# Stage a of a Fourier layer on float16 parts of x, with x read twice

## The chip, the cores and the metric

The kernel runs on one core of one Trainium2 chip. The metric is the device time of the program in microseconds (us), the median of several runs. A core has a matrix engine (TensorE, in the profile PE, with its weight loads as PEld), a vector engine (DVE), an activation engine (ACT), a general engine (POOL), and a queue engine (SP) that only issues transfers here. Each engine works through its own instructions in order; where one needs another's result, it waits on a semaphore. Transfers between HBM and the on-chip memory (SBUF) run on 16 DMA engines and are issued from SP, ACT and POOL. Matmuls write to PSUM, from where ACT or DVE fetch their results.

## The reference

Two layers follow each other. The first works on `x` of 8 batches, 3072 rows, 256 columns; the second is a feed-forward layer on its output.

```python
X = np.fft.rfft(x, axis=1)
Yr = X.real @ w_r - X.imag @ w_i + b_r
Yi = X.real @ w_i + X.imag @ w_r + b_i
Y  = soft_threshold(Yr, 0.01) + 1j * soft_threshold(Yi, 0.01)
a  = np.fft.irfft(Y, n=3072, axis=1)                  # float32, 8 x 3072 x 256
h  = np.maximum(np.maximum(a @ w1, a @ w2), a @ w3)   # 768 columns
out = h @ w_out                                       # 24576 x 256
```

The feed-forward weights come as float64 and the result is float32.

## The kernel before

**Products in parts.** Most products are made on float16 parts: a value is scaled by a power of two, its rounded float16 is the high part, what is left the low part, and `mm3` (L131) makes three matmuls, high by high, high by low and low by high. The helpers `split` (L119) and `split_scaled` (L124) make the parts: ACT writes the high one, DVE subtracts it to get the low one. `split_scaled` takes a scale, which may be a number or a column of SBUF.

**The transform.** 3072 is 96 times 32. *Stage a* (L427) is the transform over 96: for each batch, `x` is read in eight loads of four of the 32 sub-sequences (`load_x`, L398; 96 partitions by 1024 columns, 384 KB). Each load makes two products of 96 rows by 512 columns with the 96 x 96 table. ACT fetches them into `aq`, and a transfer stores `aq` in a scratch tensor `a_d` in HBM. For batches 2 to 7, the parts of `x` are `xh` and `xl` in float32r, a 32-bit type of the matrix engine, and the table's parts `fh` and `fl` are float32r too; batches 0 and 1 use plain float32 with `fr`. *Stages b, w and q* take the result in 12 pieces per batch: `load_a` (L454) reads a piece `aj` from `a_d`, `split_a` (L459) makes its float16 parts with the scale `s0x`, then come the rest of the transform (`px`), the weights `w_r` and `w_i` (`py`), bias and threshold, and the first step back (`pz`), which is stored in the scratch `z_d`.

**The scales.** `s0x` depends on the largest absolute value of `x` in the batch. DVE takes it half a load at a time in `split_x` (L416), just ahead of that half's split, and at the end of `stage_a` of the batch's last load (L441 to L452) `exponent_of` makes one number of the 16 maxima: a reduction (`col`), a matmul that spreads it over the partitions (`pt`, L209), a second reduction, and small operations on a column of 128. `power` (L221) makes scales of it in three small operations each.

**The feed-forward loop.** It runs over 8 batches, 8 chunks `c` of 384 rows and 6 blocks `f` of 128 of the 768 columns. One turn is a slot: a batch has 48. In a slot, `up` makes 18 matmuls into three PSUM tiles `pu`, and ACT and DVE make the maximum of the three and its parts `hh`; `down` makes 9 matmuls into `pd` on the `hh` of the turn before. Once per chunk the next chunk's `zq` is read, split and transformed back (`pi`). Batch 0's transform runs ahead of the loop (0 to about 137 us); batch 1's runs within the loop's batch 0, and so on.

**What sets the order.** The work of the transform is put between the turns by a list of events with a position in slots (L688 to L702), and after each turn everything up to the present slot is called. For a load `q` with number `i` in batch `b`, the load of `x` is called at `p - 3`, the split at `p` and stage a at `p + 1`. For batches 2 to 7, `p` is 48 (b - 2) + 6 i + 2: its stage a runs two batches ahead of its feed-forward turns, and its stages b to q one batch ahead. Batch 1's pieces come every 2.2 slots, from slot 8 of the loop's batch 0 on, later batches' every 2.8. The order in which the calls are made gives each instruction its priority; a scheduler at build time makes each engine's list from it and gives out buffers, so that an instruction whose buffer isn't free is passed by others. `issue_after` (L401) keeps a load of `x` behind the last load of `aj` on SP's queue. `xq`, `xh` and `xl` have two buffers each.

Of the kernel before, what the change touches and what calls it, by code (L numbers as in the profile page):

```python
# [10 lines left out]
F32R = mybir.dt.float32r  # L11
F16 = mybir.dt.float16
U32 = mybir.dt.uint32
AX = mybir.AxisListType
AF = mybir.ActivationFunctionType
ALU = mybir.AluOpType
# [3 lines left out]
LAM = 0.01  # L20
SB, SG = 10, 20
T_SCALE, Y_SCALE, H_SCALE, Q_SCALE = 2.0**-15, 2.0**-14, 2.0**-22, 2.0**12


def dft_tables():
# [68 lines left out]
def fourier_maxout_kernel(  # L94
    ctx: ExitStack, tc: tile.TileContext, x, w_r, w_i, b_r, b_i, w1, w2, w3, w_out, fa, ga, mb, mq, ident, out
):
    nc = tc.nc
    NB, S, D = x.shape
    FF = w1.shape[1]
    P = 128  # L100
    N1, N2 = 96, 32
    KD = D // P
    NF = FF // P
    NQ = 4
    NCH = N2 // NQ
    NT = NQ * N1
    NJP = 12
    SLOTS = NCH * NF
    NATIVE = 2 * NCH

    const = ctx.enter_context(tc.tile_pool(name="const", bufs=1))
# [5 lines left out]
    st = {}  # L117

    def split(hi, lo, src):  # L119
        h = hi if hi.dtype == F16 else hi.bitcast(F32)  # L120
        nc.scalar.activation(out=hi, in_=src, func=AF.Copy)
        nc.vector.tensor_tensor(out=lo, in0=src, in1=h, op=ALU.subtract)

    def split_scaled(hi, lo, src, scale):  # L124
        h = hi if hi.dtype == F16 else hi.bitcast(F32)
        nc.scalar.activation(out=hi, in_=src, func=AF.Copy, scale=scale)  # L126
        nc.vector.scalar_tensor_tensor(  # L127
            out=lo, in0=src, scalar=scale, in1=h, op0=ALU.mult, op1=ALU.subtract
        )

    def mm3(o, lh, ll, rh, rl, start=True, stop=True, **kw):  # L131
        nc.tensor.matmul(o, lh, rh, start=start, stop=False, **kw)  # L132
        nc.tensor.matmul(o, lh, rl, start=False, stop=False, **kw)  # L133
        st["mm"] = nc.tensor.matmul(o, ll, rh, start=False, stop=stop, **kw)  # L134
# [4 lines left out]
    def ff_tile(name):  # L139
        tag = spare[0]  # L140
        if len(spare) > 1:
            spare.append(spare.pop(0))
        return ps.tile([P, 512], F32, name=name, tag=tag, bufs=2 if tag == "dn" else 3)

    fr = const.tile([N1, 96], F32, name="fr")
    fh = const.tile([N1, 96], F32R, name="fh")
    fl = const.tile([N1, 96], F32R, name="fl")
    qf = const.tile([P, 2, P], F32, name="qf")
    qh = const.tile([P, 2, P], F16, name="qh")
    ql = const.tile([P, 2, P], F16, name="ql")  # L150
# [16 lines left out]
    def quad_tile(name):  # L167
        return fft.tile([96, NQ * D], F32, name=name, bufs=1 if name == "zq" else 2)
# [4 lines left out]
    def x_tile(name):  # L173
        return fft.tile([P, 2 * D], F32, name=name, bufs=2)
# [25 lines left out]
    def small(name, dt=F32, bufs=1):  # L200
        return fft.tile([P, 1], dt, name=name, bufs=bufs)


    def exponent_of(mx, name, bits, mask, low):
        rows = mx.shape[0]
        col = small("col", bufs=2)
        nc.vector.tensor_reduce(out=col[0:rows], in_=mx, axis=AX.X, op=ALU.max)
        pt = ff_tile("pt")
        nc.tensor.matmul(  # L209
            pt[:, 0:rows], col[0:rows].broadcast_to([rows, P]), id_sb[0:rows, 0:rows],  # L210
            start=True, stop=True,
        )
        e = small("e" + name, U32, 2)
        nc.vector.tensor_reduce(out=e.bitcast(F32), in_=pt[:, 0:rows], axis=AX.X, op=ALU.max)
        nc.vector.tensor_scalar(
            out=e, in0=e, scalar1=bits, scalar2=mask, op0=ALU.logical_shift_right, op1=ALU.bitwise_and
        )
        nc.vector.tensor_scalar(out=e, in0=e, scalar1=low, scalar2=None, op0=ALU.max)
        return e

    def power(name, e, sign, add, bufs=3):  # L221
        t = small(name, U32, bufs)
        nc.vector.tensor_scalar(out=t, in0=e, scalar1=sign, scalar2=add, op0=ALU.mult, op1=ALU.add)
        nc.vector.tensor_scalar(out=t, in0=t, scalar1=255.0, scalar2=None, op0=ALU.min)
        nc.vector.tensor_scalar(out=t, in0=t, scalar1=23, scalar2=None, op0=ALU.logical_shift_left)
        return t.bitcast(F32)
# [157 lines left out]
    def batch(b, kind):  # L384
        if (b, kind) not in st:
            if kind in "az":
                st[b, kind] = dram.tile([96, N2, D], F32, name=kind + "_d")
            else:
                w = 2 * NCH if kind == "x" else NJP
                st[b, kind] = fft.tile([P, w], F32, name="mx" + kind, bufs=3)  # L390
        return st[b, kind]
# [6 lines left out]
    def load_x(q):  # L398
# [8 lines left out]
            pairs = [xq[:, i * 2 * D:(i + 1) * 2 * D] for i in range(2)]  # L407
        st["x", q] = pairs

    def split_x(q):  # L410
        b, q4 = divmod(q, NCH)
        pairs = st.pop(("x", q))
        parts = []
        for i, xp in enumerate(pairs):
            if b:
                nc.vector.tensor_reduce(  # L416
                    out=batch(b, "x")[0:N1, 2 * q4 + i:2 * q4 + i + 1], in_=xp, axis=AX.X,
                    op=ALU.max, apply_absolute_value=True,
                )
            if q >= NATIVE:  # L420
                xh, xl = (x_tile(n).bitcast(F32R)[0:N1] for n in ("xh", "xl"))
                split(xh, xl, xp)
                xp = xh, xl
            parts.append(xp)
        st["xs", q] = parts

    def stage_a(q):  # L427
        b, q4 = divmod(q, NCH)
        aq = first_quads[q] if q < NCH else quad_tile("aq")
        for i, xp in enumerate(st.pop(("xs", q))):  # L430
          with tc.issue_after(st["gate"]) if q >= NCH + 2 and q < NATIVE else nullcontext():
            pa = ff_tile("pa")
            if q < NATIVE:
                nc.tensor.matmul(pa[0:96], fr, xp, start=True, stop=True)  # L434
            else:
                mm3(pa[0:96], fh, fl, *xp)
            nc.scalar.activation(out=aq[:, i * 512:i * 512 + 512], in_=pa[0:96], func=AF.Copy)
        (nc.scalar if b else nc.gpsimd).dma_start(
            out=batch(b, "a")[:, q4 * NQ:(q4 + 1) * NQ, :], in_=aq.rearrange("p (n d) -> p n d", n=NQ)
        )  # L440
        if b and q4 == NCH - 1:  # L441
            low, add = st["lim", "x"]
            e = exponent_of(st.pop((b, "x"))[0:N1], "x", 23, 0xFF, low)
            st[b, "sx"] = power("s0x", e, -1.0, 261.0), power("s1x", e, 1.0, add)


            m = small("mv", bufs=2)
            nc.vector.tensor_scalar(
                out=m, in0=e, scalar1=add, scalar2=st["eb"], op0=ALU.add, op1=ALU.max
            )  # L450
            nc.vector.tensor_scalar(out=m, in0=m, scalar1=230.0, scalar2=None, op0=ALU.min)
            st[b, "sv"] = power("s0v", m, -1.0, 231.0), power("s1v", m, 1.0, 11.0)  # L452

    def load_a(k):  # L454
        first = ("vl", 3) if k < NJP and k % 5 > 1 else ("aj", 2)
# [3 lines left out]
    def split_a(k):  # L459
        if k < NJP:  # L460
            return
        aj = st.pop(("a", k))
        ah = fft.tile([P, 2, D], F16, name="ah")
        al = fft.tile([P, 2, D], F16, name="al")
        split_scaled(ah, al, aj, st[k // NJP, "sx"][0])
        st["as", k] = [ah, al]


# [215 lines left out]
    def at(pos, fn, i, k=None, n=None):  # L684
        if n is None or 0 <= k < n:
            events.append((pos, len(events), fn, i))

    for q in range(NCH + 2, NB * NCH):  # L688
        b, i = divmod(q, NCH)
        p = i if b == 1 else (b - 2) * SLOTS + NF * i + 2  # L690
        at(p - 3, load_x, q)
        at(p, split_x, q)
        at(p + 1, stage_a, q)
    for b in range(1, NB):
        for k in range(-2, NJP + 1):
            p = 8 + 2.2 * (k + 2) if b == 1 else (b - 1) * SLOTS + 2.8 * (k + 2)
            for d, fn, i in (
                (0, load_a, k + 2), (0, split_a, k + 1), (1.6, finish_w, k - 1), (1, stage_b, k + 1),
                (3.2, stage_q, k - 1), (2, stage_w, k), (2.4, stage_w2, k),
            ):  # L700
                at(p + d, fn, b * NJP + i, i, NJP)
# [82 lines left out]
                nc.scalar.dma_start(out=out_v[b, c, t], in_=o)  # L784

    nc.sync.dma_start(out=fr, in_=fa)
    split(fh, fl, fr)

    def load_blocks(i):
        nc.sync.dma_start(out=mb_sb[:, :, 6 * i:6 * i + 6], in_=mb[:, :, 6 * i:6 * i + 6])  # L790
# [20 lines left out]
    for q in range(NCH):  # L811
        split_x(q)
        stage_a(q)
# [53 lines left out]
    for q in (NCH, NCH + 1):  # L867
        split_x(q)
        stage_a(q)
# [67 lines left out]
```

## Time and profile before

| | |
|---|---|
| three runs | 2063.78, 2065.49, 2070.24 us (median 2065.49) |
| the profiled execution | 2070.11 us, its span 2068.3 us |
| granted TensorE clock | 0.995 in the mean |
| busy, share of the span | PE 99%, PEld 69%, DVE 75%, ACT 50%, POOL 1% |
| HBM | 87.14 MB read, 75.50 MB written, 79 GB/s |
| loads of `xq` | 58 of 384 KB, 4.0 us from issue to landing in the median |
| `pa` on float32r | 288 matmuls of 96x96 by 512 columns |

A profile shows one execution: each instruction with its line, engine, tiles (out<-in), start and duration. A row of a group has the count, the busy time, the mean duration, then the idle time of the engine just before such instructions and what ended it ("<-DVE c L758 1.1" is 1.1 us that ended with DVE's result of line 758). Matmuls overlap, so their durations add up to more than the time; what counts is how far apart they start. "issue" is waiting for which the profile shows no cause. A row of the waits has the total, the number and the longest. A wait is put down to what came last.

### The profile page before, as it was taken

The numbers are of one execution on the slowest core, as the hardware profiler recorded it, in microseconds if no ns is written. First come the engines' busy times: TensorE is split into PE (matmuls) and PEld (weight loads), VectorE is DVE, ScalarE is ACT, GpSimd is POOL, SyncE is SP. The second block draws the span as 40 slices with busy tenths as digits, with TensorE's granted clock in tenths as the row PEclk, the third lists the DMA queues.
The fourth block names the chain that finished last, engine by engine and source line by source line (L and its number), as shares of the span: only waits on it lengthen the run. The fifth ranks groups of instructions, "written<-read, shape, count | busy, mean of one in ns | idle before, by whom it ended". The sixth has DMA issues, their size and how long they took to land.

```text
span 2068.3 us, 38435 instructions
## 1 busy us (share of the span) xinstructions
PE 2040.7 (99%) x15500; PEld 1431.4 (69%) x15500; DVE 1547.9 (75%) x3043; ACT 1035.0 (50%) x2051; POOL 27.6 (1%) x79
## 2 busy tenths in 40 slices
PE   8999999999999999999999999999999999999998
PEld 5756766677776767767776777767777777776666
DVE  3987897678867888678886788767887578865543
ACT  4755554455545555455554455445554445433333
POOL 1000000000000000000000000000000000000000
PEclk9999999999999999999999999999999999999999
DMA  9454221322213222223213222132221212111100
GB/s 311 141 155 123 90 70 52 107 68 89 75 52 100 79 84 62 65 83 92 85 60 97 62 78 87 47 100 72 86 74 44 77 52 67 42 47 32 34 30 23
DMA packets 106694, 165.13 MB, mean 80 GB/s; under 512 B 9795, under 2 KB 85059, under 8 KB 106419
## 3 DMA queue, kind: packets, MB, share of 16 engines
q1 hardware_dynamic: 45347, 86.69, 14.4%
q10 hardware_dynamic: 60032, 72.37, 10.6%
q0 software_dynamic: 1136, 3.61, 0.5%
q8 instruction: 121, 1.98, 0.4%
q14 instruction: 58, 0.48, 0.1%
HBM read 87.14 MB, written 75.50 MB: 79 GB/s over the span
## 4 chain that ended last, share of the span: by engine, by line
PE 82%; DVE 10%; DMA 3%; ACT 2%; issue 2%; ACTq 0%; SPq 0%; DVEq 0%
PE pu L134 16%; PE pu L132 16%; PE pu L133 16%; PE pd L134 5%; PE pd L132 5%; PE pd L133 5%; PE py L132 2%; PE py L133 2%; PE py L134 2%; DMA xq<-in_x_dram 2%; DVE u L620 1%; PE pi L132 1%; PE pa L434 1%; DVE h L760 1%; PE pa L133 1%
## 5 line engine op out<-in xcount | busy, mean ns | idle before, releaser
L132 PE MATMUL pu<-yh,wuh 128*128 128x384 f16 x2304 | 752.6, 327 | 2.2 <-DVE c L758 1.1
L133 PE MATMUL pu<-yl,wuh 128*128 128x384 f16 x2304 | 751.7, 326 | 0.0
L134 PE MATMUL pu<-yh,wul 128*128 128x384 f16 x2304 | 751.7, 326 | 0.0
L126 ACT ACTIVATE hh<-h 128x384 f16<-128x384 f32 x384 | 200.4, 522 | 512.3 <-DVE h L760 509.8
L134 PEld LDWEIGHTS <-wul 128*128 128x128 f16 x2304 | 225.5, 98 | 148.9 <-issue 1.1
L132 PEld LDWEIGHTS <-wuh 128*128 128x128 f16 x2304 | 225.9, 98 | 143.4 <-issue 14.7
L133 PEld LDWEIGHTS <-wuh 128*128 128x128 f16 x2304 | 225.9, 98 | 135.1 <-issue 5.8
L758 DVE TENSOR_TENSOR c<-pu,c 128x384 f32<-128x384 f32 x384 | 212.5, 554 | 136.8 <-PE pu L134 76.3
L127 DVE SCALAR_TENSOR_TENSOR hh<-h,hh 128x384 f16<-128x384 f32 x384 | 213.6, 556 | 135.3 <-ACT hh L126 132.0
L134 PE MATMUL pd<-woh,hh 128*128 128x256 f16 x1152 | 313.6, 273 | 0.9 <-DVE hh L127 0.8
L132 PE MATMUL pd<-woh,hh 128*128 128x256 f16 x1152 | 313.9, 273 | 0.4 <-ACT hh L126 0.3
L133 PE MATMUL pd<-wol,hh 128*128 128x256 f16 x1152 | 313.8, 273 | 0.0
L760 DVE TENSOR_TENSOR h<-pu,c 128x384 f32<-128x384 f32 x384 | 212.7, 554 | 45.6 <-PE pu L134 33.8
L757 ACT ACTIVATE c<-pu 128x384 f32<-128x384 f32 x384 | 186.0, 484 | 102.7 <-PE pu L134 98.6
L620 DVE SCALAR_TENSOR_TENSOR u<-py,s1x,cs 64x256 f32<-64x256 f32 x308 | 148.5, 482 | 40.9 <-ACT cs L631 30.9
L132 PE MATMUL py<-wch,tt 128*128 128x256 f16 x504 | 137.4, 273 | 0.4 <-DVE yl L127 0.4
L134 PE MATMUL py<-wch,tt 128*128 128x256 f16 x504 | 137.4, 273 | 0.0
L133 PE MATMUL py<-wcl,tt 128*128 128x256 f16 x504 | 137.4, 273 | 0.0
L132 PEld LDWEIGHTS <-hh 128*128 128x128 f16 x1152 | 112.7, 98 | 34.3 <-ACT hh L126 1.0
L133 PEld LDWEIGHTS <-hh 128*128 128x128 f16 x1152 | 112.7, 98 | 33.4
L783 ACT ACTIVATE o<-pd,s1u 128x256 f32<-128x256 f32 x192 | 83.6, 469 | 90.9 <-PE pd L134 53.3
L134 PEld LDWEIGHTS <-hh 128*128 128x128 f16 x1152 | 112.7, 98 | 15.3 <-DVE hh L127 2.0
(205 smaller groups left out, 2889.6 us busy)
## 6 DMA issues: line engine op xcount, KB each, us to landing
aj<-a_d SPq DMA_DIRECT2D x96, 256.0 KB, 2.8
z_d<-zs ACTq DMA_DIRECT2D x96, 256.0 KB, 2.1
out_dram<-o ACTq DMA_DIRECT2D x192, 128.0 KB, 2.1
zq<-z_d SPq DMA_DIRECT2D x63, 384.0 KB, 3.5
xq<-in_x_dram SPq DMA_DIRECT2D x58, 384.0 KB, 4.0
a_d<-aq ACTq DMA_DIRECT2D x56, 384.0 KB, 3.0
rw<-in_moe_w_dram SPq DMA_DIRECT2D x6, 768.0 KB, 9.4
xr<-in_x_dram SPq DMA_DIRECT2D x6, 384.0 KB, 11.4
```

The costliest lines, as they stand in the source:

```text
L126: nc.scalar.activation(out=hi, in_=src, func=AF.Copy, scale=scale)
L127: nc.vector.scalar_tensor_tensor(out=lo, in0=src, scalar=scale, in1=h, op0=ALU.mult, op1=ALU.subtract)
L132: nc.tensor.matmul(o, lh, rh, start=start, stop=False, **kw)
L133: nc.tensor.matmul(o, lh, rl, start=False, stop=False, **kw)
L134: st["mm"] = nc.tensor.matmul(o, ll, rh, start=False, stop=stop, **kw)
L434: nc.tensor.matmul(pa[0:96], fr, xp, start=True, stop=True)
L620: nc.vector.scalar_tensor_tensor(out=u[64 * c:64 * c + 64, j], in0=pk[r], scalar=inv[r], in1=c1[r], op0=ALU.mult, op1=ALU.add,)
L757: nc.scalar.activation(out=c1, in_=pu[0], func=AF.Copy)
L758: nc.vector.tensor_tensor(out=c1, in0=pu[1], in1=c1, op=ALU.max)
L760: nc.vector.tensor_tensor(out=h32, in0=pu[2], in1=c1, op=ALU.max)
L783: nc.scalar.activation(out=o, in_=pd[t], func=AF.Copy, scale=st[b, "su"][1])
```

## The change

For batches 2 to 7, stage a works on float16 parts. The table's parts `fh` and `fl` become float16, made with a scale of 2^10. `xh` and `xl` become float16, made by `split_scaled` with a new scale `sx2` in a column, which needs the batch's maximum ahead of the first split. So `x` is read twice: once for the maximum (`load_x`, `largest_x`), and once more for the split. The two halves of a load take one buffer of the tiles `xh` and `xl` each, with high and low part side by side. For b of 3 to 7 the maximum is called at slot 48 (b - 3) + 6 i + 5, between the splits of the batch before, and its load three slots earlier. For batch 2 it is called at slots 8, 10, ... 22, and the split, which stood at slots 2, 8, ... 44, at 24.5, 27.4, ... 44.8. The scales of a batch (`scale_x`) are made behind the last maximum, not behind the last stage a. `aq` is fetched with a scale of 2^-17, so what lies in `a_d` is scaled already, and `aj` of batches 2 to 7 is split without one. Batches 0 and 1 stay on float32.

```diff
+A_SCALE, F_SCALE = 2.0**-17, 2.0**10
...
-    fh = const.tile([N1, 96], F32R, name="fh")
-    fl = const.tile([N1, 96], F32R, name="fl")
+    fh = const.tile([N1, 96], F16, name="fh")
+    fl = const.tile([N1, 96], F16, name="fl")
...
+    def largest_x(q):
+        b, q4 = divmod(q, NCH)
+        for i, xp in enumerate(st["x", q]):
+            nc.vector.tensor_reduce(
+                out=batch(b, "x")[0:N1, 2 * q4 + i:2 * q4 + i + 1], in_=xp, axis=AX.X,
+                op=ALU.max, apply_absolute_value=True,
+            )
+        if b > 1 and q4 == NCH - 1:
+            scale_x(b)
+
+    def scale_x(b):
+        low, add = st["lim", "x"]
+        e = exponent_of(st.pop((b, "x"))[0:N1], "x", 23, 0xFF, low)
+        st[b, "sx"] = power("s0x", e, -1.0, 261.0), power("s1x", e, 1.0, add)
+        if b > 1:
+            st[b, "sx2"] = power("s2x", e, -1.0, 268.0)
...
     def split_x(q):
         b, q4 = divmod(q, NCH)
-        pairs = st.pop(("x", q))
+        if b == 1:
+            largest_x(q)
         parts = []
-        for i, xp in enumerate(pairs):
-            if b:
-                nc.vector.tensor_reduce(
...
+        for i, xp in enumerate(st.pop(("x", q))):
             if q >= NATIVE:
-                xh, xl = (x_tile(n).bitcast(F32R)[0:N1] for n in ("xh", "xl"))
-                split(xh, xl, xp)
+                t = x_tile(("xh", "xl")[i]).bitcast(F16)[0:N1]
+                xh, xl = t[:, 0:2 * D], t[:, 2 * D:4 * D]
+                split_scaled(xh, xl, xp, st[b, "sx2"][0:N1])
                 xp = xh, xl
...
-            nc.scalar.activation(out=aq[:, i * 512:i * 512 + 512], in_=pa[0:96], func=AF.Copy)
+            nc.scalar.activation(
+                out=aq[:, i * 512:i * 512 + 512], in_=pa[0:96], func=AF.Copy,
+                scale=1.0 if q < NATIVE else A_SCALE,
+            )
...
-        split_scaled(ah, al, aj, st[k // NJP, "sx"][0])
+        if k // NJP > 1:
+            split(ah, al, aj)
+        else:
+            split_scaled(ah, al, aj, st[k // NJP, "sx"][0])
...
-        p = i if b == 1 else (b - 2) * SLOTS + NF * i + 2
+        p = i if b == 1 else 24.5 + 2.9 * i if b == 2 else (b - 2) * SLOTS + NF * i + 2
+        if b > 1:
+            m = 8 + 2 * i if b == 2 else (b - 3) * SLOTS + NF * i + 5
+            at(m - 3, load_x, q)
+            at(m, largest_x, q)
         at(p - 3, load_x, q)
         at(p, split_x, q)
         at(p + 1, stage_a, q)
...
-    split(fh, fl, fr)
+    split_scaled(fh, fl, fr, F_SCALE)
```

More of the change, by code (lines that the diff above doesn't have):

```diff
@@ L408, in load_x @@
         st["x", q] = pairs
+    def largest_x(q):
[13 more added lines that the diff above has]
+            st[b, "sx2"] = power("s2x", e, -1.0, 268.0)
+        m = small("mv", bufs=2)
+        nc.vector.tensor_scalar(
+            out=m, in0=e, scalar1=add, scalar2=st["eb"], op0=ALU.add, op1=ALU.max
+        )
+        nc.vector.tensor_scalar(out=m, in0=m, scalar1=230.0, scalar2=None, op0=ALU.min)
+        st[b, "sv"] = power("s0v", m, -1.0, 231.0), power("s1v", m, 1.0, 11.0)
     def split_x(q):
         b, q4 = divmod(q, NCH)
-        pairs = st.pop(("x", q))
+        if b == 1:
+            largest_x(q)
         parts = []
-        for i, xp in enumerate(pairs):
-            if b:
[L416 to L419, printed above, removed]
+        for i, xp in enumerate(st.pop(("x", q))):
             if q >= NATIVE:
-                xh, xl = (x_tile(n).bitcast(F32R)[0:N1] for n in ("xh", "xl"))
-                split(xh, xl, xp)
+                t = x_tile(("xh", "xl")[i]).bitcast(F16)[0:N1]
+                xh, xl = t[:, 0:2 * D], t[:, 2 * D:4 * D]
+                split_scaled(xh, xl, xp, st[b, "sx2"][0:N1])
                 xp = xh, xl
@@ L436, in stage_a @@
                 mm3(pa[0:96], fh, fl, *xp)
-            nc.scalar.activation(out=aq[:, i * 512:i * 512 + 512], in_=pa[0:96], func=AF.Copy)
+            nc.scalar.activation(
+                out=aq[:, i * 512:i * 512 + 512], in_=pa[0:96], func=AF.Copy,
+                scale=1.0 if q < NATIVE else A_SCALE,
+            )
         (nc.scalar if b else nc.gpsimd).dma_start(
@@ L440, in stage_a @@
         )
[L441 to L452, printed above, removed]
+        if b == 1 and q4 == NCH - 1:
+            scale_x(b)
     def load_a(k):
```

## The prediction

> **What bounds the kernel now.** I read the page's busy shares first, then the chain of waits, then the windows by batch, and last the groups and the timeline around stage a.
>
> ```profile
> span 2068.3 us, 38435 instructions
> PE 2040.7 (99%) x15500; PEld 1431.4 (69%) x15500; DVE 1547.9 (75%) x3043; ACT 1035.0 (50%) x2051; POOL 27.6 (1%) x79
> ...
> PE 82%; DVE 10%; DMA 3%; ACT 2%; issue 2%; ACTq 0%; SPq 0%; DVEq 0%
> ```
>
> TensorE has work in 99% of the span and is 82% of the chain that ended last; the 10% of DVE lie where a late DVE result came through to a matmul. So a second that leaves TensorE's queue is worth a second, and one that leaves or joins DVE, ACT or a DMA queue is worth something only where it makes TensorE wait. Where that happens is in the windows by batch of the feed-forward loop:
>
> ```profile
> 137.00:376.00 239.00, 234.26 (x1775) 161.68 (x1774) 190.81 (x374) 123.41 (x249) 2.16 (x8) 0.98 0.30 90
> 376.00:624.00 248.00, 247.63 (x1943) 175.54 (x1942) 195.55 (x379) 128.74 (x257) 2.91 (x8) 1.00 0.25 77
> ...
> 1371.00:1620.00 249.00, 248.23 (x1946) 175.64 (x1945) 194.62 (x376) 129.04 (x258) 2.12 (x8) 1.00 0.25 75
> ```
>
> The columns are length, then busy time of PE, PEld, DVE, ACT and POOL, the granted clock, the DMA share and GB/s. While the loop runs batch 0 (137 to 376) TensorE idles 239.00 - 234.26 = 4.7 us at a clock of 0.98; while it runs batches 1 and 5 it idles 0.4 and 0.8 us. From batch 1 on there are hardly any stalls to win; matmul time alone can be won there. In the first window both matter.
>
> **Part 1, the matmuls of stage a.** 48 loads of x (batches 2 to 7) give two products each, each of three matmuls of 512 columns: 288 matmuls, now on float32r, then on float16. What counts is their pace, start to start, in a run of them:
>
> ```profile
> 622.33 0.40 PE L133 MATMUL pa<-xl,fh 96*96 96x512 f32 x1
> 622.57 0.39 PE L134 MATMUL pa<-xh,fl 96*96 96x512 f32 x1
> 622.80 0.39 PE L132 MATMUL pa<-xh,fh 96*96 96x512 f32 x1
> 623.03 0.40 PE L133 MATMUL pa<-xl,fh 96*96 96x512 f32 x1
> 623.26 0.40 PE L134 MATMUL pa<-xh,fl 96*96 96x512 f32 x1
> ```
>
> ```profile
> 600.02 0.38 PE L132 MATMUL pz<-vp,qh 128*128 128x512 f16 x1
> 600.23 0.38 PE L133 MATMUL pz<-vp,qh 128*128 128x512 f16 x1
> 600.45 0.38 PE L134 MATMUL pz<-vp,ql 128*128 128x512 f16 x1
> 600.66 0.21 PE L132 MATMUL pi<-ga_sb,zh 96*128 96x96 f16 x1
> ```
>
> The float32r matmuls follow each other at (623.26 - 622.33) / 4 = 0.2325 us, float16 ones of as many columns at (600.66 - 600.02) / 3 = 0.2133 us. The difference, 0.0192 us, times 288 is **5.5 us** off TensorE's queue. Bounds: 0, if the pace of the 96-row, 96-column product isn't due to its type, and 5.5. The row nearest in type and columns is pz, so I take the whole.
>
> The Trainium skill, page "TensorE: Matmul & The Clock Gate", section "Wait — 56ns, not 53.3ns?", gives a warm matmul its columns over 2.4 GHz and some 2.5 ns, 215.7 ns for 512; pz in the trace has 213 ns at the 10 ns steps of the timeline, which agrees. By the page's figure the term would be 288 x 0.0168 = 4.8 us and the time 2059.3.
>
> The change of type also has an exit:
>
> ```profile
> 711.52 0.40 PE L134 MATMUL pa<-xh,fl 96*96 96x512 f32 x1
> ...
> 711.76 0.10 PEld L132 LDWEIGHTS <-ah 128*128 128x128 f16 x1 [0.30 <-issue]
> ...
> 711.95 0.22 PE L132 MATMUL px<-mb_all,ah 128*128 128x128 f16 x1
> ```
>
> ```profile
> L132 PEld LDWEIGHTS <-ah 128*128 128x128 f16 x336 | 32.9, 98 | 5.4 <-issue 1.5
> ```
>
> Behind the last float32r matmul the next weights are loaded only when it has streamed (711.76), where float16 weights are loaded a matmul ahead, and the next product starts 0.43 us after it in place of 0.2325: 0.19 us lost. The group's 1.5 us of "issue" at 0.30 each make 5 such places, **1.0 us**. The other 43 groups are followed by a longer product that hides most of it; I give them 0.01 each, **0.4 us** (an estimate, a tick of the timeline). Bounds of the exits: 0 to 1.4.
>
> **Part 2, the splits.** xh and xl become float16 with a scale that stands in a column; aj's split loses such a scale for 72 of its 84 pieces.
>
> ```profile
> L416 DVE TENSOR_REDUCE mxx<-xq 96x1 f32<-96x512 f32 x112 | 74.2, 675 | 17.7 <-DMA xq<-in_x_dram 17.5
> ...
> L122 DVE TENSOR_TENSOR xl<-xq,xh 96x512 fp32r<-96x512 f32 x96 | 65.2, 684 | 18.3 <-ACT xh L121 18.3
> L127 DVE SCALAR_TENSOR_TENSOR al<-aj,s0x,ah 128x512 f16<-128x512 f32 x84 | 62.7, 747 | 5.1 <-ACT ah L126 3.4
> ...
> L126 ACT ACTIVATE ah<-aj,s0x 128x512 f16<-128x512 f32 x84 | 60.0, 716 | 7.2 <-DMA aj<-a_d 4.8 <-PE px L133 2.3
> L121 ACT ACTIVATE xh<-xq 96x512 fp32r<-96x512 f32 x96 | 58.6, 620 | 3.8 <-DMA xq<-in_x_dram 3.8
> ```
>
> The scaled split of 512 elements costs 716 on ACT and 747 on DVE, the plain one 620 and 684. DVE: 96 x 63 ns more and 72 x 63 ns less, 1.5 us over six batches; ACT: 24 x 96 ns, 2.3 us. The maxima stay 96 of 675 ns. The new scale is three small operations per batch, like the one below:
>
> ```profile
> L224 DVE TENSOR_SCALAR s0x<-s0x x7: 148/150/152, 169.1 to 1621.7; 128x1 uint32<-128x1 uint32 x7
> ```
>
> 18 x 150 ns are 2.7 us. All of it lies under TensorE: DVE has 248.00 - 195.55 = 52 us free in a batch, ACT 119. I cost it at **nothing**; without the cover it would be the 1.5 + 2.7 us of DVE. The split of the 96 x 96 table at the start is one operation for one.
>
> **Part 3, what moves in time.** The maximum of batch b (3 to 7) moves from its split, a batch earlier (slots 5 to 47 of the 48 before). So from batch 1 on each window does as many maxima as before, three slots away from the splits instead of in one burst with them. The first window does batch 2's and batch 3's: 16 x 0.675 = 10.8 us more on DVE, 190.81 + 10.8 = 201.6 of 239, 84% in place of 80%. The last window with splits has 10.8 us less. The share is far from 100%, so on average nothing is due; locally see the rivals.
>
> Batch 2's splits move from slots 2, 8, ... 44 to 24.5, 27.4, ... 44.8. With them go the only two waits of stage a on TensorE's side worth speaking of:
>
> ```profile
> L132 PE MATMUL pa<-xh,fh 96*96 96x512 f32 x96 | 41.8, 437 | 3.5 <-ACT zs L675 2.4 <-DVE u L620 1.1
> ```
>
> ```profile
> 274.03 0.47 PE L132 MATMUL pa<-xh,fh 96*96 96x512 f32 x1 [2.37 <-ACT zs L675]
> ...
> 277.66 0.43 PE L134 MATMUL pu<-yh,wul 128*128 128x384 f16 x1
> 277.93 0.33 PE L132 MATMUL pu<-yh,wuh 128*128 128x384 f16 x1
> ```
>
> ```profile
> 260.00:280.00 20.00, 17.63 (x117) 11.29 (x115) 16.72 (x33) 10.50 (x21) 0.00 (x0) 0.91 0.19 60
> ```
>
> They are 3.5 us of idle time, and the longer one was followed by a halved clock (a mean of 0.91 over 20 us, 1.8 us lost; the durations fall back at 277.9). That makes 5.3 us. Whether eight denser places meet such waits no row shows: the lower bound is that both vanish, -5.3; the upper that more come, priced in the rivals. Two in eight is the only rate I have, so I take as many again: **0**.
>
> The scale's matmul pt now follows the last maximum at once, on TensorE's queue ahead of the next up products. It could wait there for DVE. The group says how that goes for the other scales, which are made so already:
>
> ```profile
> L209 PE MATMUL pt<-id_sb,col 128*128 128x128 f32 (+1 forms) x38 | 7.5, 285 | 0.1
> ```
>
> 0.1 us of waiting over 38 of them: I take **0**; the upper bound is six waits of the 1.1 us that DVE u cost above, 6.6 us.
>
> 48 more loads stand on SP's queue, behind them the loads of aj and zq, and the second load of x may keep ACT waiting as the first keeps DVE.
>
> ```profile
> xq<-in_x_dram SPq DMA_DIRECT2D x58, 384.0 KB, 4.0
> ```
>
> ```profile
> SPq L406 <- DVE xl L122: 206.2, 12, 27.8
> ```
>
> They are asked for three slots, some 15 us, ahead of use and land in 4.0. SP already stands up to 27.8 us before such a load for its buffer without a stall of that length anywhere on TensorE, and 48 x 384 KB over the 1480 us from 137 to 1620 add 13 GB/s to 77. The maxima's 17.5 us of waits for x stood on DVE; as much again on ACT would fall in its free half. **0**; without that cover it is a second 17.5 us.
>
> **The sum.** 5.5 + 1.0 + 0.4 = 6.9 us. The profiled execution took 2070.1 us (span 2068.3, 1.8 around it), so it would take 2063.2. It is the slow end of the runs shown; their median is 2065.5, and from that the forecast is **2058.6 us**, -0.33%.
>
> **The rivals.** *The stalls go too* (20%). Both waits of the first window belong to places that batch 2 leaves, and the burst of maximum and subtraction is parted: 6.9 + 5.3 = 12.2, 2053.3 us. Against it: the new places lie where batch 1's stages are densest.
>
> *It doesn't do what it says* (17%): the pace of 0.2325 belongs to 96 columns and 96 rows or to the reading of weights, not to the type. Then 0 to 1.4 remains, 2064 to 2065.5 us. For it: no row has a float16 product of 96 x 96 by 512. Against it: pa's 512 columns also last longer one by one than pz's, 403 ns against 363, and the type is what the two differ in beside 32 rows:
>
> ```profile
> L133 PE MATMUL pa<-xl,fh 96*96 96x512 f32 x96 | 38.7, 403 | 0.3 <-DVE xl L122 0.3
> ...
> L133 PE MATMUL pz<-vp,qh 128*128 128x512 f16 (+1 forms) x91 | 33.0, 363 | 0.0
> ```
>
> The Trainium skill, same page, section "Weight-path perf modes — Fast Weight Load (FWL) and DoubleRow", has the fast load for 128 columns of weights only, which these never have; no run so far shows it for float16.
>
> *DVE is too full in the first window* (13%, slower). Batch 2's places come every 2.9 slots while batch 1's products come every 2.2, and all share DVE:
>
> ```profile
> 200.00:220.00 20.00, 18.89 (x164) 13.51 (x162) 19.12 (x37) 10.83 (x22) 0.00 (x0) 1.00 0.26 74
> ...
> 280.00:300.00 20.00, 20.00 (x178) 14.92 (x177) 19.09 (x36) 12.06 (x24) 0.00 (x0) 1.00 0.36 107
> ```
>
> Where DVE is at 95% today, the window at 200 lost 1.1 us and that at 280 nothing. Each pa that then waits for its PSUM buffer behind a late zs costs 2.4 + 1.8 = 4.2 us with the clock's fall. The two of today cost 5.3; to eat the 6.9 it takes 12.2 / 4.2, three of the eight places. At five: 21.0 - 5.3 - 6.9 = +8.8, 2074.3 us. Against it: DVE goes to 84% only, and ends the window with slack. On the clock the Trainium skill, same page, section "What's actually happening", has it halved after an idle window of some 3.4 us; here 2.4 us of waiting were enough, and the measured row decides. By the page's length such a wait would cost no clock, and five would come to 12.0 - 5.3 - 6.9, 2065.3 us.
>
> **How the numbers follow.** Forecast 45%, own range 2055 to 2062; the rest beyond the rivals' 50%, 5%, is that pt or the x loads take some us off the gain. A measurement of this kernel can tell about 0.3%, 6.2 us: faster is under 2059.3, slower over 2071.7. The forecast is faster in some six of ten of its own cases (0.27), stalls that go are faster (0.20), and a little of the rest: 0.49. Slower is the third rival and a part of the rest: 0.14. The remaining 0.37 is no difference. The range from 2050 to 2068 leaves out the third rival's far part and the best tail.
>
> **What would show it.** pa on TensorE at 96x512 f16 with means near 363 and starts 0.213 apart (part 1); no 0.30 of "issue" at the weights that follow pa (exits); xh near 716, xl near 747, ah near 620, al near 684 (part 2); DVE near 202 us in the loop's first window, and the idle time of pa's first matmul there (part 3); pt's idle time near 0. The prediction is wrong if pa keeps its 0.23, or if TensorE's idle time in the first window leaves 3 to 7 us.

## The result

The changed kernel takes a median of 2117.3 us (2116.7 to 2121.0, 4 runs), the kernel before 2067.0 us on the same chip (2063.8 to 2070.2, 4 runs). The ratio is 1.0238, with a 95% interval of 1.0226 to 1.0251: it is **slower by 50 us**, where 2058.6 and a range of 2050 to 2068 were forecast.

The busy shares and the chain of waits of the changed kernel:

```profile
span 2119.2 us, 38519 instructions
PE 2056.9 (97%) x15500; PEld 1432.2 (68%) x15500; DVE 1548.5 (73%) x3061; ACT 1037.6 (49%) x2051; POOL 24.5 (1%) x79
...
PE 70%; DVE 13%; DMA 8%; ACT 4%; issue 3%; ACTq 1%; SPq 1%; DVEq 0%
```

DVE and ACT do no more than before (DVE 1548.5 against 1547.9 us, ACT 1037.6 against 1035.0), and TensorE has as many matmuls (15500). What has grown are the shares of DMA (3 to 8%) and DVE (10 to 13%) in the chain that ended last, at TensorE's cost (82 to 70%). The windows by batch, with the columns as in the prediction, and behind them 20 us in the middle of a batch:

```profile
137.00:376.00 239.00, 229.89 (x1747) 158.22 (x1748) 199.51 (x406) 124.52 (x246) 2.17 (x8) 0.99 0.40 116
376.00:624.00 248.00, 241.22 (x1868) 168.93 (x1867) 190.27 (x366) 125.15 (x249) 2.12 (x8) 0.98 0.29 86
624.00:873.00 249.00, 241.60 (x1859) 169.38 (x1858) 190.83 (x372) 125.19 (x248) 2.12 (x8) 0.98 0.30 89
1371.00:1620.00 249.00, 244.55 (x1899) 171.67 (x1898) 182.88 (x357) 127.90 (x253) 0.00 (x0) 0.99 0.25 75
...
770.00:790.00 20.00, 16.55 (x112) 11.02 (x113) 13.37 (x25) 10.31 (x20) 0.00 (x0) 0.83 0.18 54
```

In the windows of loop batches 0 to 5 TensorE now idles 4 to 10 us (before 0.3 to 4.7), and the granted clock is 0.98 to 0.99; before it was 0.98 in the first of them and 1.00 in the others. The loss lies in all the batches, not in the first window: from the first up product of one batch to that of the next, loop batches 0 to 5 took 270.8, 248.5, 249.3, 248.5, 249.8 and 249.2 us before, and 273.6, 259.1, 259.5, 261.8, 258.3 and 254.3 after. A wait of TensorE can be taken from the starts of two matmuls in a row, as the time beyond the usual step of their shape. Added up behind 200 us, the waits of over 0.25 us come to some 49 us (12 before), and 14 stretches of 3.4 us run at half the clock (1 before), which costs another 21 us (2 before). The products of stage a are some 5 us shorter. 37 + 19 - 5 = 51 us, and the spans differ by 50.9.

The waits that have grown, in the list of waits (in all, times, longest, in us), after:

```profile
DVE xh L128 <- ACT xh L127: 30.7, 25, 3.5
PE pi L133 <- DVE u L641: 24.9, 12, 4.0
ACT xh L127 <- DMA xq<-in_x_dram: 22.8, 11, 3.8
DVE mxx L414 <- DMA xq<-in_x_dram: 21.4, 24, 2.3
PE px L133 <- ACT zs L696: 9.1, 4, 3.0
```

and the same of before, where `px` waits for no `zs`:

```profile
DVE xl L122 <- ACT xh L121: 18.3, 36, 1.1
DVE mxx L416 <- DMA xq<-in_x_dram: 17.5, 18, 2.4
ACT xh L121 <- DMA xq<-in_x_dram: 3.8, 2, 2.3
PE pi L132 <- DVE u L620: 1.3, 3, 0.6
```

One of the longest is followed here in the changed kernel's timeline (start, duration, engine, line, operation; in brackets the idle time before it and what ended it):

```profile
765.32 0.38 SPq L475 DMA_DIRECT2D aj<-a_d  x1
765.79 0.42 SPq L407 DMA_DIRECT2D xq<-in_x_dram  x1
...
770.89 0.72 ACT L127 ACTIVATE xh<-xq,s2x 96x512 f16<-96x512 f32 x1 [3.38 <-DMA xq<-in_x_dram]
...
771.64 0.75 DVE L128 SCALAR_TENSOR_TENSOR xh<-xq,s2x,xh 96x512 f16<-96x512 f32 x1 [3.55 <-ACT xh L127]
772.32 1.99 DVE L641 SCALAR_TENSOR_TENSOR u<-py,s1x,cs 64x256 f32<-64x256 f32 x4
...
773.34 0.26 PE L133 MATMUL pi<-ga_sb,zh 96*128 96x96 f16 x1 [3.75 <-DVE u L641]
...
774.60 0.53 PE L133 MATMUL pu<-yh,wuh 128*128 128x384 f16 x1
...
780.30 0.33 PE L133 MATMUL pu<-yh,wuh 128*128 128x384 f16 x1
```

Read it from below. TensorE stands 3.75 us before `pi`, since `u` comes late; `u` stands on DVE's list behind the split `xh`, which waits for ACT's half of it, which waits for a load of x. That load was issued 5.1 us before, at once behind the load of `aj` (L402 ties it there, and `aj` waits for `al` to free its buffer). ACT and DVE work off their lists in order, so all that stands behind the split waits too, though it needs no x. Then the clock falls: `pu` lasts 0.53 us in place of 0.33, from 1.3 us before TensorE goes on until 778.9, and the window of 770 to 790 has a granted clock of 0.83.

### The profile page after: what moved, and what is told of

The parts are those of the page before. It is cut to its first block, busy times and chain, and to the rows that moved or that the text cites. A ratio compares the mean times of both kernels' runs of the same rounds, so it can differ in the third digit from the quotient of the medians.

```text
span 2119.2 us, 38519 instructions
## 1 busy us (share of the span) xinstructions
PE 2056.9 (97%) x15500; PEld 1432.2 (68%) x15500; DVE 1548.5 (73%) x3061; ACT 1037.6 (49%) x2051; POOL 24.5 (1%) x79
## 4 chain that ended last, share of the span: by engine, by line
PE 70%; DVE 13%; DMA 8%; ACT 4%; issue 3%; ACTq 1%; SPq 1%; DVEq 0%
PE pu L135 14%; PE pu L134 14%; PE pu L133 14%; PE pd L135 5%; PE pd L133 5%; PE pd L134 5%; DMA xq<-in_x_dram 4%; DVE u L641 2%; PE py L135 2%; PE py L133 2%; PE py L134 2%; DMA aj<-a_d 1%; DVE c L783 1%; DVE h L785 1%; DMA a_d<-aq 1%
```

## The experiments

Each is told with its edit (against the changed kernel, or against the one before where that is said), what was expected, and its median with that of the kernel before, run beside it. Behind it stand the ratio and its 95% interval.

**One read.** The first read of x and the maxima of batches 2 to 7 go; the scales are batch 1's, so that part of the computation is left out.

```diff
-        if b > 1:
-            st[b, "sx2"] = power("s2x", e, -1.0, 268.0)
+        st[b, "sx2"] = power("s2x", e, -1.0, 268.0)
...
+        for n in range(2, NB):
+            for name in ("sx", "sx2", "sv"):
+                st[n, name] = st[1, name]
...
-            at(m - 3, load_x, q)
-            at(m, largest_x, q)
```

> The changed kernel without the first read of x and without the maxima of batches 2 to 7, which this leaves out: the scales made for batch 1 serve for all. Stage a on float16, the scaled splits and their places stay. Theory Q (a load of x lands late because it stands on SP behind a load of aj, and ACT or DVE then stand in order before TensorE's next need): half of the late loads are gone and the buffers of xq serve one stream, so most of the 50 us go; 2060 to 2085 us, with waits of xh for the load left where it still stands behind aj. Rival D (DVE too full, or the scaled splits too long): the DVE work of the maxima, 65 us, is gone, so it falls below 2060 us as well, but xh no longer waits for anything. Rival F (the float16 products or the wait for the new scale cost the time): it stays near 2117 us.

2073.8 us against 2065.9, ratio 1.0035 (1.0022 to 1.0048). Some 42 of the 50 us go with the read and its maxima, and no wait behind 200 us brings a stretch at half the clock, but it isn't faster than before even with 96 maxima less. Waits of the same kind stay in this kernel's list:

```profile
ACT xh L127 <- DMA xq<-in_x_dram: 24.3, 16, 3.6
PE pi L133 <- DVE u L643: 10.6, 11, 2.8
```

So the second read isn't the whole of it: the splits still stand right behind their loads.

**No tie behind aj.** The loads of x of batches 2 to 7 are no longer kept behind that of `aj`.

```diff
-        with tc.issue_after(st["ld"].ins) if q >= NCH + 2 else nullcontext():
+        with tc.issue_after(st["ld"].ins) if NCH + 2 <= q < NATIVE else nullcontext():
```

> The changed kernel, where the loads of x of batches 2 to 7 are no longer tied behind the last load of aj on SP's queue; two buffers of xq as before. Theory Q: the loads go out when their buffer is free, some 5 us earlier at the place where one was issued at 765.8 us, and the five waits of pi of 3.7 to 4.2 us with the halved clock behind them go: 2058 to 2075 us. Rival B (two streams share two buffers, and that makes the load late): no more than a few us, 2105 to 2117 us. Rival D and F: 2117 us.

2081.3 against 2065.9, 1.0070 (1.0055 to 1.0085): some 35 of the 50 us come back with nothing left out and both reads in place. That is 6 us more than theory Q allowed. ACT's `xh` no longer appears as waiting for a load, and one stretch of half clock remains. The edit also lets the lists of SP, DVE and ACT come out in another order.

**Float32r, else as changed.** `fh`, `fl`, `xh` and `xl` go back to float32r, and with that to four buffers for a load: one of `xh` and one of `xl` for each half.

```diff
-    fh = const.tile([N1, 96], F16, name="fh")
-    fl = const.tile([N1, 96], F16, name="fl")
+    fh = const.tile([N1, 96], F32R, name="fh")
+    fl = const.tile([N1, 96], F32R, name="fl")
...
-                t = x_tile(("xh", "xl")[i]).bitcast(F16)[0:N1]
-                xh, xl = t[:, 0:2 * D], t[:, 2 * D:4 * D]
+                xh, xl = (x_tile(n).bitcast(F32R)[0:N1] for n in ("xh", "xl"))
```

> The changed kernel with the parts of x and of the table in float32r, and all else as changed: two reads, the places, the scale, aj split without one. Theory Q and rival B: the time stays high, 2117 us and the 5 to 7 us that the float16 products save, 2118 to 2130 us. Rival F (float16): back to 2067 us.

2087.4 against 2065.9, 1.0099 (1.0082 to 1.0116): 29 us less than the changed kernel, with *longer* products, where 2118 to 2130 was expected. The edit has two parts, the type and the buffers; the run below parts them.

**The second read in other buffers.** It goes to the eight raw buffers that hold x at the start, in place of the two of `xq`.

```diff
-    def load_x(q):
+    def load_split_x(q):
+        load_x(q, q >= NATIVE)
+
+    def load_x(q, again=False):
...
-            if 2 <= q < NCH:
+            if again or 2 <= q < NCH:
...
-        at(p - 3, load_x, q)
+        at(p - 3, load_split_x, q)
```

> The changed kernel, where the second read of x goes into the eight buffers of the tile raw, idle after the weights are made, so that the two reads share no buffer; the tie behind aj stays. Theory Q: a load still goes out only behind a load of aj, but an earlier one, where the missing buffer had held it to the next: part of the 50 us goes, 2070 to 2110 us. Rival B: all of it goes, 2055 to 2070 us. Rival D and F: 2117 us.

2125.9 against 2065.9, 1.0281 (1.0265 to 1.0296): no better, some 10 us worse, and above every time that was expected. The wait is the same one under another name:

```profile
ACT xh L127 <- DMA xr<-in_x_dram: 23.2, 10, 4.2
```

That two reads share two buffers of `xq` isn't the cause. With eight buffers at hand the load still stands behind `aj`.

**Float16, four buffers.** The changed kernel with its types, but each half of a load with one buffer of `xh` for its high part and one of `xl` for its low part, half of each unused.

```diff
-                t = x_tile(("xh", "xl")[i]).bitcast(F16)[0:N1]
-                xh, xl = t[:, 0:2 * D], t[:, 2 * D:4 * D]
+                xh, xl = (x_tile(n).bitcast(F16)[0:N1, 0:2 * D] for n in ("xh", "xl"))
```

> The changed kernel on float16, with the high part in a buffer of xh and the low part in one of xl for each half, as the kernel before has it, so that a load takes four buffers and not two; the lists of SP, ACT and DVE are then those of the run on float32r with two reads (2087.4 us). Theory P (the halved use of the buffers let the list put a split behind a load just issued, and the type has no part in it): 2087 less the 5 to 7 us of the products, 2079 to 2083 us. Rival F (float16 itself costs time): 2100 to 2117 us.

2085.5 against 2065.5, 1.0100 (1.0083 to 1.0117), as the float32r kernel with as many buffers (and 2.5 us above what was expected). The lists of SP, ACT and DVE are the same in these two, instruction by instruction, so those 29 to 30 us belong to **the buffers**, not to the type. The timeline of the float32r one shows what they do, at the place of the wait followed above:

```profile
742.88 0.41 SPq L407 DMA_DIRECT2D xq<-in_x_dram  x1
...
753.55 0.72 ACT L127 ACTIVATE xh<-xq,s2x 96x512 fp32r<-96x512 f32 x1
...
759.77 0.22 PE L133 MATMUL pi<-ga_sb,zh 96*128 96x96 f16 x1 [1.41 <-DVE u L640]
```

With two buffers of a name and two halves to a load, the next split has to wait until the last load's products are through, and the build-time list puts it late: 10.7 us behind its load, which has long landed (3.7 us is the median to landing). In the changed kernel a load takes one buffer of each name, so the other one is there for the next load, and the list puts the split earlier: 5.1 us behind a load that the tie has made late. Over all 48 loads for the splits (each matched to its split in the order of the calls), 23 splits of the changed kernel start within 6 us of their load's issue, 8.7 us in the median. With four buffers none does: 32 us in the median, 10 at least.

**Float16 by a fixed scale, in the kernel before.** x is read once, as before; `xh` and `xl` are float16 with a fixed scale of 2^10 in place of the batch's own, once with the halved buffers of the change (shown), and once with four. `fh` and `fl` become float16 by the same scale, and `aq` is fetched with 2^-20.

```diff
-                xh, xl = (x_tile(n).bitcast(F32R)[0:N1] for n in ("xh", "xl"))
-                split(xh, xl, xp)
+                t = x_tile(("xh", "xl")[i]).bitcast(F16)[0:N1]
+                xh, xl = t[:, 0:2 * D], t[:, 2 * D:4 * D]
+                split_scaled(xh, xl, xp, 2.0**10)
```

> The kernel before, with stage a of batches 2 to 7 on float16 parts alone: x is read once and its maximum taken at the split as before, and the parts are made with a fixed scale of 2^10 in place of one from the maximum, so it serves only for x of about this size (that part of the computation is left out). aj's split keeps its scale. If the products' pace is what float16 gives (0.2155 us in place of 0.232, and no exit), 288 products save 5 to 7 us and nothing moves: 2059 to 2062 us against 2066. If the two halves of a load, which now take one buffer of xh and xl each, let the splits run ahead to a load just landed, as theory Q has it for the changed kernel, waits of xh or of the maximum for the load grow and eat it: 2065 to 2085 us.

> The kernel before, with stage a of batches 2 to 7 on float16 parts by a fixed scale of 2^10 (so it serves only for x of about this size, that part of the computation is left out), x read once, and high and low part in a buffer of xh and xl each as before. The lists of SP, ACT and DVE are then in the order of the kernel before, instruction for instruction. Theory P: the products' pace and the exits alone change, 5 to 7 us less than before's 2066: 2058 to 2062 us. If float16 has a cost of its own that the lists don't show (the scaled split of DVE, the weights' loads): 2064 to 2075 us.

Halved: 2087.6 against 2065.5, 1.0107 (1.0090 to 1.0124), a little above its second range. Four: 2069.4 against 2066.1, 1.0019 (1.0007 to 1.0031). The buffers alone cost some 19 us (1.0107 against 1.0019) in a kernel that reads x once, with the same wait as above in the list of the halved one:

```profile
ACT xh L126 <- DMA xq<-in_x_dram: 31.5, 21, 4.1
PE pi L132 <- DVE u L622: 15.9, 11, 3.9
```

The other half of this result is a riddle: with four buffers, shorter products and no second read, it is 3 us slower than before, not faster. In its trace TensorE's waits of over 0.25 us come to some 18 us, 6 more than before: about what the products save.

**Both causes undone together.** The changed kernel with four buffers and without the tie.

> The run with four buffers per load on float16, and the loads of x of batches 2 to 7 no longer tied behind a load of aj. If both causes add up, the late loads of both streams are gone: 2060 to 2072 us. If the tie and the buffers are two ways to the same lateness, it stays where each of them alone brings it: 2079 to 2083 us.

2071.6 against 2065.5, 1.0032 (1.0019 to 1.0045): 44 of the 50 us come back. `pi` still waits for `u`, but 1.6 us at most:

```profile
PE pi L133 <- DVE u L640: 8.5, 12, 1.6
```

**Earlier loads.** Both reads in the raw buffers and called nine slots ahead in place of three (the maxima of batch 2: three), with the tie and the halved buffers kept, and then with four buffers and without the tie.

```diff
-            at(m - 3, load_x, q)
+            at(m - (3 if b == 2 else 9), load_split_x, q)
...
-        at(p - 3, load_x, q)
+        at(p - (9 if b > 1 else 3), load_split_x, q)
```

> The changed kernel, with both reads of batches 2 to 7 in the eight buffers of raw and each load called nine slots ahead of its use in place of three (three as before for the maximum of batch 2); the tie behind aj stays. Theory Q: the loads are tied to a load of aj some two pieces earlier, land long before use, and the waits for x vanish from ACT and DVE: 2055 to 2072 us. If the place of the splits and of the maxima between the other work is the cause, and not the loads: 2080 to 2117 us with no waits for x.

> The changed kernel with all three cures: high and low part in a buffer each, both reads of batches 2 to 7 in the eight buffers of raw, called nine slots ahead of use (batch 2's maximum three), no tie behind aj. Theory Q and P: no load of x is late any more, the time is that of four buffers without the tie (2071.6 us) less the waits for x left there: 2062 to 2070 us. If the places of the work alone make the rest: 2070 to 2080 us, with no waits for x.

2097.0 against 2065.5, 1.0157 (1.0142 to 1.0173); and 2071.0 against 2066.1, 1.0024 (1.0015 to 1.0033). Earlier loads win 19 us. In the first of the two no split waits for x any more, and yet it is 31 us over before, as the second theory had it, and `pi` waits for `u` nearly as long as in the changed kernel:

```profile
PE pi L133 <- DVE u L644: 20.8, 12, 3.8
```

Ahead of its wait at 763.6 us, at the place followed above, the chain of waits holds no load of x from 715 us on. It goes to and fro between ACT and DVE over the split and the work beside it, with `u` behind them. So a split that stands early delays `u` by its place as well, and not only by a late load. With the other two undone as well earlier loads win next to nothing more (5 us over before, against 6), so late loads of the second read aren't what remains.

**The tie alone.** The kernel before without it, and the fixed-scale float16 kernel with four buffers without it (the edit is that of the second run).

> The kernel before, where the loads of x of batches 2 to 7 are no longer tied behind a load of aj, and nothing else. Theory Q: the wait of pi in each batch, 0.4 to 0.7 us, and the load of x on the chain before it go: 2060 to 2066 us, 0 to 5 us less than before. If the tie does no harm to the kernel before: 2066 us, or more if a load of aj or zq is now late behind x.

> The kernel before with stage a of batches 2 to 7 on float16 by a fixed scale (x read once; for x of about this size alone, the scale from the maximum being left out for the parts), high and low part in a buffer each, and the loads of x of batches 2 to 7 not tied behind a load of aj. In the run without this last edit the chain of waits at the wait of pi goes al, load of aj, load of x (5.4 us), mxx, u, pi. Theory Q: that chain takes up what the products save, and without the tie the 5 to 7 us of the products come through: 2057 to 2063 us. If something else takes them up: 2065 to 2070 us.

2072.9 and 2073.3 against 2067.0, 1.0025 (1.0015 to 1.0034) and 1.0022 (1.0011 to 1.0033). Both are slower than theory Q had it. In the kernel before, the tie is worth 5 to 6 us; without it TensorE's waits of over 0.25 us go from some 12 to some 16 us. Again float16 makes no difference between two kernels that are alike but for it.

**Without the maxima, in both types.** Where does the float16 products' gain go? The chain of waits of the fixed-scale kernel with four buffers (start, duration, what) has this ahead of a `pi`:

```profile
740.51 0.76 DVE al L127
...
741.29 0.38 SPq L458
...
741.72 5.44 DMA xq<-in_x_dram
...
747.18 1.27 DVE mxx L416 x2
...
748.92 0.39 DVE u L621
...
749.87 0.22 PE pi L132
```

No matmul stands in it: `al` frees a buffer, `aj` is loaded, x behind it, then the maxima, `u` and `pi`. TensorE comes to that place earlier and waits. If this chain takes the gain up, the gain must appear when DVE needn't wait for x. So the maxima of batches 2 to 7 are left out of both kernels, with batch 1's scales in their place; the lists of SP, ACT and DVE are the same in the two.

```diff
-            if b:
+            if b == 1:
                 nc.vector.tensor_reduce(
...
+            for n in range(2, NB):
+                for name in ("sx", "sv"):
+                    st[n, name] = st[1, name]
```

> The kernel before, without the maxima of x of batches 2 to 7: their columns take the scales of batch 1, so that part of the computation is changed, and VectorE has 36.5 us (48 pieces by 0.68 us of the maximum's row, some of it off the path) less to do and never stands still for a late x by itself. Theory A (the chain of al, load of aj, load of x behind it, maximum, u, pi sets the end of a batch in the kernel before as well): 4 to 10 us under the kernel before, so 2056 to 2063. Theory B (TensorE's own queue sets the end, and the maxima are covered): within 2 us of the kernel before.

> The kernel that reads x once and multiplies float16 parts by a fixed scale, four buffers to a load, likewise without the maxima of batches 2 to 7; the lists of SP, ACT and VectorE are the same as in its partner in float32r. Theory A (float16's shorter products are worth nothing only because the chain through the load of x and the maximum ends as late as they do): 4 to 6 us under its partner, the whole of the shorter products. Theory B (something else takes the products' gain up, at the evictions after them or on the chain of the splits): within 2 us of its partner, and the waits of pi or px longer by about what the products save.

2062.3 us (float32r) and 2058.4 us (float16) against 2065.6: ratios 0.9985 (0.9976 to 0.9993) and 0.9967 (0.9955 to 0.9980). Float16 is now 4.0 us faster, and every run of it (2056.9 to 2059.9) lies below every run of the other (2060.4 to 2065.2). The maxima in float32r are worth 3.3 us, between the two theories (4 to 10, or within 2); there are 96 of them, 64 us of DVE, not the 36.5 that the expectation names. The windows of a batch and the waits at `pi`, float32r first:

```profile
376.00:624.00 248.00, 246.95 (x1936) 174.42 (x1935) 183.75 (x342) 128.56 (x257) 2.13 (x8) 1.00 0.24 75
...
PE pi L132 <- DVE u L623: 4.1, 5, 1.0
```

```profile
376.00:624.00 248.00, 246.70 (x1941) 173.89 (x1940) 184.42 (x343) 128.58 (x257) 2.12 (x8) 1.00 0.25 77
...
PE pi L132 <- DVE u L624: 4.5, 5, 1.1
```

With equal waits at `pi` the shorter products come through; with the maxima those waits went from 1.3 us in all in the kernel before to 6.6 in its float16 counterpart. None of these loads of x is in the middle part (380 to 1640 us) of the chain of these two kernels, and there were four of over 4 us in that of before. So the gain is taken up where the maxima stand, in the kernels with the tie. Whether it is the maxima's wait for x or DVE's 64 us of their work isn't parted by these runs: the untied kernels also wait there.

## Why the prediction was wrong

**"A second that leaves TensorE's queue is worth a second", and one that joins another queue only where TensorE waits.** This premise carried the sum, and its two halves failed. A second off TensorE's queue was worth nothing with the maxima in place, and what changed on the other queues made TensorE wait 37 us more. TensorE's 99% of busy time doesn't say that nothing else ends as late: by the chains of waits, `al`, `aj`, x, the maxima and `u` run along it with hardly any slack. (That the maxima have to do with it is shown; which link of that chain binds isn't.) The evidence was at hand. The chain of waits of the kernel before lists loads of x where, by the premise, there should have been matmuls:

```profile
630.10 5.42 DMA xq<-in_x_dram
...
746.16 4.54 DMA xq<-in_x_dram
...
1132.50 5.88 DMA xq<-in_x_dram
...
1493.93 4.33 DMA xq<-in_x_dram
```

I read the shares of that chain, took DMA's 3% as small, and didn't look at where they lay.

**Part 1, the pace: right in size, worth nothing in place.** In the changed kernel's timeline the products follow each other at 0.22 us, in place of 0.2325:

```profile
724.16 0.38 PE L133 MATMUL pa<-xh,fh 96*96 96x512 f16 x1
724.38 0.38 PE L134 MATMUL pa<-xh,fh 96*96 96x512 f16 x1
724.60 0.38 PE L135 MATMUL pa<-xh,fl 96*96 96x512 f16 x1
724.82 0.38 PE L133 MATMUL pa<-xl,fh 96*96 96x512 f16 x1
```

(724.82 - 724.16) / 3 = 0.22 at the timeline's ticks; over all products of stage a the median step is 215 ns, and in the kernel before 233 (steps under 0.3 us). 288 x 0.018 = 5.2 us, where I had 5.5 from three steps of `pz`, whose median over the whole trace of before is 216 ns and not 213. The Trainium skill ("TensorE: Matmul & The Clock Gate", section "Wait — 56ns, not 53.3ns?") gives 215.7 ns for 512 columns, which agrees with both. The rival that the type has nothing to do with it falls. 4.0 us of the gain show where DVE doesn't do the maxima, 0 to -3 elsewhere.

**The exits: not confirmed.** The 0.30 of "issue" ahead of the weights of `ah` isn't the type's. In the fixed-scale float16 kernel with four buffers, `px` starts 509 ns behind the start of the last `pa` product (median of the five places), where it was 429 in the kernel before. It waits some 100 ns longer, about what six shorter products save: something else sets when it starts.

**Part 2, the splits: every duration right.** The groups of the changed kernel:

```profile
L123 DVE TENSOR_TENSOR al<-aj,ah 128x512 f16<-128x512 f32 x72 | 49.5, 688 | 8.3 <-ACT ah L122 7.9
L122 ACT ACTIVATE ah<-aj 128x512 f16<-128x512 f32 x72 | 44.9, 624 | 19.6 <-DMA aj<-a_d 16.4 <-PE px L134 3.3
L128 DVE SCALAR_TENSOR_TENSOR xh<-xq,s2x,xh 96x512 f16<-96x512 f32 x48 | 35.7, 744 | 30.7 <-ACT xh L127 30.7
L127 ACT ACTIVATE xh<-xq,s2x 96x512 f16<-96x512 f32 x48 | 34.4, 716 | 31.7 <-DMA xq<-in_x_dram 22.8 <-DVE s2x L226 8.3 <-ACT c L782 0.2
```

716, 744, 624 and 688 ns against the 716, 747, 620 and 684 forecast. But "nothing" was reckoned from the sum of DVE's free time, and the part that mattered isn't in it: the edit also put high and low part of a half into one buffer, so that a load takes two and not four. The text of the change says so, and no step of the prediction asked what a buffer more does to the list. Undone by itself it gives 30 of the 50 us back.

**Part 3, the loads on SP: "0; without that cover it is a second 17.5 us".** This is the step that failed by name. The cover was that x lands 4.0 us after its issue, and is asked for three slots ahead; but it is issued when `aj` lets it, and the splits aren't tied to slots. On ACT 22.8 us of waiting for x came (11 waits), near the price named for the case without cover, and I had put them into ACT's free half. They didn't fall there, since ACT's list is in order and DVE's splits, `u` and `pi` hang on it. Untying the loads by itself brought 35 us back, issuing them earlier 19. The buffers' 30 and the tie's 35 overlap, since together they bring 44: a late load hurts where a split stands right behind it.

**The first window and pt.** DVE has 199.5 us there (202 forecast), and its batch took 2.8 us longer. The rival that DVE is too full there was the only one on the slower side, and it named the wrong place and the wrong cause: the other five batches lost 48. The scale's matmul `pt` waits 0.1 us in all, as taken. DMA went from 77 to 86 to 89 GB/s, by the 13 forecast at most.

**The clock.** The price of "2.4 + 1.8 us" for a wait was of the right kind: 37 us more of waits cost some 19 more by the clock.

**What stays open.** With both causes undone the changed kernel is 6 us over before (1.0032), at twelve waits for `u`. But the kernel before without its tie is nearly as far over (1.0025), and so is its float16 counterpart (1.0022): between untied kernels with four buffers, no cost of the second read or of the scaled splits is clear of the noise. With the tie the same two float16 kernels lie 20 us (two reads) and 3 us (one) over before, so what comes with the second read is dear behind the tie. That may be its loads, the new place of the maxima or the splits with a scale in a column (716 and 744 ns against 620 and 684); no run parted them. Why untying by itself costs the kernel before 5 to 6 us stays open too.

## What to carry to other kernels

A busy share of 99% on one engine doesn't make its work the bound: look into the chain of waits for pieces of other engines or DMAs that lie on it, for these have no slack there either and can take up what the busy engine saves. When an edit changes how many buffers a step takes, even downward, it can change the order that a build-time list gives to in-order engines; ask what an instruction placed earlier will stand waiting for, and who stands behind it. A load's latency counts from when its queue lets it go, so find what the load is tied behind before calling it hidden.

## What was unexpected of the hardware

How short a wait of TensorE brings the half clock. Over the 16 traces of this case, behind 200 us of the span and short of its end, 16 waits were longer than 3 us, and in each or right behind it began one or two stretches of 3.4 us at half the clock. Of 35 waits of 1.9 to 2.9 us, 18 had one; of the shorter ones, none. In the float32r kernel with both reads, twelve waits of 1.0 to 2.4 us, 19 us in all, cost no clock; in the changed kernel 13 waits of 1.5 to 4.1 us, 37 us in all, cost some 21 more. So waiting costs half as much again or nothing, by how it is cut. The Trainium skill ("TensorE: Matmul & The Clock Gate", section "What's actually happening") has the clock fall after an idle window of some 3.4 us, watched by a window that runs freely: the stretches' length agrees, and waits well under it were enough here.
